# Two-level gates of an attention and feed-forward kernel: another order of the seven products, sums on VectorE, weights' sums at other places

## The chip, the cores and the metric

One core of one Trainium2 chip runs the whole kernel in one launch. The metric is device time in microseconds (us) of an execution, as the median of several runs. TensorE (PE in the profile) multiplies, VectorE (DVE), ScalarE (ACT) and GpSimd (POOL) work on whole tiles, and SyncE (SP) issues most of the transfers.

## The reference

All arrays are float32. Attention without softmax comes first, on 8 batches of 8 heads, 576 tokens and 64 columns; then a feed-forward network on the 4608 tokens.

```python
kv = np.einsum('bhsd,bhse->bhde', k, v)
out = np.einsum('bhsd,bhde->bhse', q, kv)
rms = np.sqrt(np.mean(out * out, axis=-1, keepdims=True) + 1e-06)
x = (out / rms * g_norm)           # heads side by side: 4608 x 512
a = x @ w1                         # 512 x 1024
b = x @ w2                         # 512 x 1024
return ((a * b @ w3) @ w_out)      # 1024 x 1024, then 1024 x 512
```

The kernel multiplies w3 and w_out with each other first, so that only the two gates' products (with w1 and w2) and one product with the folded matrix remain for each token.

## The kernel before

**Groups.** The tokens go through the network in nine groups of 512. Groups 0 to 6 are the first 512 tokens of batches 0 to 6; then comes group 8, the 64 left-over tokens of all batches together, and group 7 is last. Attention for the next group is spread over the current one: a list of steps is called at fixed places (`between`), twice for each of the four quarters `p` of the gate's columns. Places are counted from 0 within a group; at places 1 and 4 stand attention's own products (kv, then q with kv, and the normalisation: L333, L416, L384, L385, L394).

**Products.** Every large product is cut by Winograd's form of Strassen's scheme: seven products of half-size blocks in place of eight, with sums of blocks before (s1 to s4 of the one factor, t1 to t4 of the other) and sums of products behind. In the gates of groups 0 to 6 the scheme is used once (`winograd`, L618). In groups 8 and 7, which `TWICE` names, quarters 0 and 1 of the gates are computed together with the scheme used on two levels (`gates_of_two`, from L824): each of the seven products (`products(n, w, ...)`, L850) is itself seven products of 128 x 128 blocks, kept in two PSUM banks, and the stretch is gone through twice, once for w1 (`w` = 0) and once for w2 (`w` = 1). Quarters 2 and 3 use one level. The product with the folded matrix (`project_twice`, L1049) always uses two.

**The stretch of two levels.** `products(n, ...)` with `new` true starts the banks afresh; with false it adds onto what they hold. Banks are `r1`, `r2` (of five that PSUM keeps under `mm`) and `r3` (of three under `at`). `keep` copies two banks to SBUF by two ScalarE copies (L863, L864); a product that adds onto the same banks has to wait for these copies. `add` is two VectorE additions of banks to a kept tile (L868, L869). `finish` makes one quarter of a gate's block out of seven kept pieces by four VectorE additions (L880 to L883), and in the second pass multiplies it onto the first pass's result (L885). L902 adds the kept `u3` to `p5`.

**What follows.** `sum_ab_two` makes the sums s1, s2, s3, s4 of quarters 0 and 1 as four wide operations of 128 x 512, on GpSimd (L911 to L914). They are needed by `project_twice`. The gates of quarter 3 run at the same time (PE L618; VectorE L757 and L758 once for each of the blocks c12, c22 and c11, L671, L672); behind c11, L1007 to L1011 (`sum_inner`) make the inner sums for the first product of `project_twice`.

**The weights' sums.** The two-level gates need sums of the weights' blocks, seven sets of three (L775, L776, L777: 128 x 256 each, on VectorE). `prepare_w` makes them in groups 3 and 4 and stores each set with three transfers (L780) to `w_l2` in DRAM. It alternates between two buffers, so a set can be written only when the set before the last has been stored. It is called at places 0 to 3 of both groups.

**Who decides the order.** PE, GpSimd and SP run in the order in which the program issues their work. ScalarE's order and, outside of the last quarter and `project_twice` (and `gates_of_two`), VectorE's are arranged by a scheduler. Every engine works its own list strictly in order.

Of the kernel before, what the change touches and what calls it, by code (L numbers as in the profile page):

```python
# [3 lines left out]

# [18 lines left out]
def kernel(  # L23
# [32 lines left out]
    nc = tc.nc  # L56
# [19 lines left out]
    ps_mm = ctx.enter_context(tc.tile_pool(name="ps_mm", bufs=5, space=PSUM))  # L76
# [531 lines left out]
    def late_tile(name):  # L608
        return late_pool.tile([P, 7, P], FP32, name=name[0] if name[0] == "u" else name)
# [214 lines left out]
    def gates_of_two(T):  # L824

        if not places:
            other = work.tile([P, 2, 2, NP // 2, N], FP32, name="xT")
            other = other.rearrange("p i j r n -> p (i j r n)")
            places.extend([other[:, 0:PART // 2], other[:, 1024:1024 + PART // 2]])
            other = work.tile([P, 2, 2, 4, D], FP32, name="xn", bufs=1)  # L830
            places.append(other.rearrange("p i l m d -> p (i l m d)")[:, 0:PART // 2])
            places[:] = [t.rearrange("p (n t) -> p n t", t=P) for t in places]

        def products(n, w, ps, new):
            a_name, b_name = PRODUCTS[n]
            a11, a12, s3, a22 = (t[:, w] for t in w_blocks(a_name))
            s1, s2, s4 = (
                loaded_w[q // 7][:, q % 7 * 2 * P + w * P:q % 7 * 2 * P + (w + 1) * P]
                for q in range(3 * n, 3 * n + 3)
            )  # L840
            b11, _, b21, b22 = (
                xb[T][b_name][:, c, i * P:(i + 1) * P] for c in range(2) for i in range(2)
            )
            t1, t2, t3, t4 = x_sums[n]
            seen = set()
            for place, x, y in (
                (0, a11, b11), (3, a12, b21), (1, a22, t4), (2, s1, t1), (6, s2, t2), (5, s4, b22),
                (4, s3, t3),
            ):
                nc.tensor.matmul(  # L850
                    ps[place // 4][:, place % 4, :], lhsT=x, rhs=y,
                    start=new and place // 4 not in seen, stop=True, skip_group_check=True,
                )
                seen.add(place // 4)
            if w == 1 and n in (2, 4, 6):
                load_b()
            return ps

        def banks(pool, tag):
            return [bank(pool, tag).rearrange("p (i n) -> p i n", n=P) for _ in range(2)]  # L860

        def keep(t, ps):
            nc.scalar.copy(t[:, 0:4], ps[0])  # L863
            nc.scalar.copy(t[:, 4:7], ps[1][:, 0:3])  # L864
            return t

        def add(z, ps):
            nc.vector.tensor_add(z[:, 0:4], ps[0], z[:, 0:4])  # L868
            nc.vector.tensor_add(z[:, 4:7], ps[1][:, 0:3], z[:, 4:7])  # L869

        def finish(z, w, i, j):

            def wide(i):
                return z[:, i:i + 1].to_broadcast([P, 2, P])

            dst = ab[i][:, 0:2, j, :].rearrange("p m (n t) -> p m n t", t=P)
            to = dst
            if w:
                to = late_pool.tile([P, 2, N], FP32, name="c").rearrange("p m (n t) -> p m n t", t=P)
            nc.vector.tensor_add(z[:, 6], z[:, 6], z[:, 0])  # L880
            nc.vector.tensor_add(z[:, 4:6], z[:, 4:6], wide(6))
            nc.vector.tensor_add(to[:, 1], z[:, 1:3], wide(4))  # L882
            nc.vector.tensor_add(to[:, 0], z[:, 3:6:2], z[:, 0:3:2])  # L883
            if w:
                nc.vector.tensor_mul(dst, dst, to)  # L885

        for w in range(2):
            r1 = products(0, w, banks(ps_mm, "mm"), True)
            p1 = keep(late_tile("p1"), r1)
            r3 = products(1, w, banks(ps_at, "at"), True)  # L890
            add(p1, r3)
            finish(p1, w, 0, 0)
            r2 = products(2, w, banks(ps_mm, "mm"), True)
            p5 = keep(places[2] if w else late_tile("p5"), r2)
            products(3, w, r1, False)
            z = keep(late_tile("u2"), r1)
            products(4, w, r2, False)
            add(z, r2)
            finish(z, w, 0, 1)
            products(5, w, r1, False)  # L900
            u3 = keep(places[0], r1)
            nc.vector.tensor_add(p5, p5, u3)  # L902
            finish(p5, w, 1, 1)
            products(6, w, r1, False)
            finish(keep(places[1], r1), w, 1, 0)
        loaded_w.clear()

    def sum_ab_two():
        c11, c12, c21, c22 = (ab[i][:, 0:2, j, :] for i in range(2) for j in range(2))
        s1, s2, s4 = (t[:, 0:2] for t in ab_sums)  # L910
        nc.gpsimd.tensor_add(s1, c12, c22)  # L911
        nc.gpsimd.tensor_sub(s2, s1, c11)
        nc.gpsimd.tensor_sub(c12, c11, c12)
        nc.gpsimd.tensor_sub(s4, c21, s2)  # L914

    def project(T, between):
        def done(name, one, two):
# [96 lines left out]
    def project_twice(T, last, ahead, load_after):  # L1014
# [147 lines left out]
    w3o_l2 = dram.tile([8, P, PART], FP32, name="w3o_l2")  # L1162
    w_l2 = dram.tile([P, 3 * PART], FP32, name="w_l2")
    PRODUCTS = [
        ("a11", "b11"), ("a12", "b21"), ("s1", "t1"), ("s2", "t2"), ("s4", "b22"), ("s3", "t3"),
        ("a22", "t4"),
    ]
    TWICE = (B, B - 1)
# [95 lines left out]
    for n, T in enumerate(groups):  # L1264
        pieces = steps(T + 1) if n + 2 < NG else iter([])

        def between():
            next(pieces, lambda: None)()
            if T == 1:
                for _ in range(2):  # L1270
                    if next(preparing, 0) == 0 and len(loaded_b) < 3:
                        load_b()
            if T in (3, 4) and p < 2:
                next(preparing_w, 0)
            if T == B - 2 and p == 2 and not replaced:
                replaced.append(True)
                replace_a21()

        if T in TWICE:
            once = iter([T])  # L1280
            gates(T, 2, lambda: [sum_x(t) for t in islice(once, 1)])
            run(sum_ab(2))
            in_order = tc.manual_schedule(engines={mybir.EngineType.DVE})
            in_order.__enter__()
            gates_of_two(T)
            sum_ab_two()
        for p in range(NF):
            if T in TWICE and p + 1 < NF:
                continue
            if T and p + 1 == NF:  # L1290
                sum_1, sum_2, sum_4, sum_3 = sum_ab(p)
                following = {
                    "c12": [], "c22": [sum_1],
                    "c11": [
                        lambda: sum_inner(0, lambda: all_of(f() for f in (sum_2, sum_3))),
                        lambda: sum_inner(1),
                    ],
                    "c21": [sum_4],
                }

                if T not in TWICE:
                    in_order = tc.manual_schedule(engines={mybir.EngineType.DVE})
                    in_order.__enter__()
                gates(T, p, between, lambda name: all_of(f() for f in following[name]))
                continue
            gates(T, p, between if T or p else lambda: None)
            if T == 0:
                if p + 1 < NF:
                    run(sum_w(p + 1))
                for n in range(2):  # L1310
                    if len(converted) < len(todo):
                        ahead = [copies["xT"] if p == 0 else copies["u3"][0], copies["u2"][p]][n]
                        with tc.issue_after(ahead.ins):
                            begin_next()
                        end_next()
                if p + 1 == NF:
                    allocate_projection()
                    run(*(f(i) for i in range(NF) for f in (sum_ab, combine_w3o)))
            else:
                run(sum_ab(p))  # L1320
        last = n + 1 == NG
        if T:
            project_twice(
                T, last, [] if last else combine_x(groups[n + 1]),
                load_w if not last and groups[n + 1] in TWICE else load_b,
            )
            in_order.__exit__(None, None, None)
            continue
        project(T, between)
        run(combine_x(1))  # L1330
        preparing, preparing_w, replaced = prepare_b(), prepare_w(), []
        third = late_pool.tile([P, 3, 2, P], FP32, name="inner_sums")
        inner_sums.append([third[:, i] for i in range(3)])
# [30 lines left out]
```

## Time and profile before

| | |
|---|---|
| median of 4 runs | 766.46 us (766.04 to 767.49) |
| the profiled execution | 767.05 us |
| its span in the trace | 765.3 us, so 1.75 us lie around it |
| PE busy | 756.2 us, 99% of the span, granted clock 0.999 |
| VectorE, ScalarE, GpSimd busy | 589.8 us, 263.3 us, 175.8 us |
| stretch of two levels, group 8 | 635.43 to 657.86 us |
| stretch of two levels, group 7 | from 704.46 to 726.89 us |

Times in the trace are counted from the span's start. In a timeline a row is: start, duration, engine, line, operation, output<-inputs, shape, count, and in brackets the engine's idle time before it with what ended it. Durations of neighbours on VectorE overlap a little, so what one operation costs in a queue is the distance from its start to the next start, not its duration. PE has two records for each matmul of float32.

### The profile page before, as it was taken

How to read it: one execution, taken by the hardware profiler on the slowest of the kernel's cores; microseconds unless marked ns; L12 is line 12 of the kernel's file. 1: busy time of each engine (PE TensorE's matmuls, PEld its weight loads, DVE VectorE, ACT ScalarE, POOL GpSimd, SP SyncE). 2: the span in 40 equal slices, each digit the busy share in tenths (PEclk: the TensorE clock that was granted, in tenths of full speed). 3: DMA queues.
4: the chain of work that ended last, by engine and by line, in shares of the span. 5: the costliest groups of instructions: out<-in, count | busy, mean ns of one | idle time of the engine just before them, and what ended most of it. 6: DMA issues, size and time to landing. Idle time of an engine off the chain costs nothing.

```text
span 765.3 us, 15018 instructions
## 1 busy us (share of the span) xinstructions
PE 756.2 (99%) x5943; PEld 661.4 (86%) x5943; DVE 589.8 (77%) x1159; ACT 263.3 (34%) x499; POOL 175.8 (23%) x198
## 2 busy tenths in 40 slices
PE   8999999999999999999999999999999999999998
PEld 6455788888899889988998899889988999999997
DVE  7978999548978468967786688467776778997897
ACT  6677763213221332232222322322223213322421
POOL 0000000222510442044104320431053124206020
PEclk9999999999999999999999999999999999999999
DMA  9996541238998835694569456835642460465234
GB/s 317 340 352 195 185 144 37 84 96 251 330 274 279 233 102 166 213 263 143 167 206 276 118 164 225 223 92 168 227 119 64 152 226 20 147 209 181 95 134 144
DMA packets 137050, 140.84 MB, mean 184 GB/s; under 512 B 77076, under 2 KB 124308, under 8 KB 136980
## 3 DMA queue, kind: packets, MB, share of 16 engines
q1 hardware_dynamic: 134528, 125.46, 54.7%
q10 hardware_dynamic: 2452, 14.42, 5.5%
q8 instruction: 47, 0.77, 0.4%
q14 instruction: 23, 0.19, 0.1%
HBM read 105.78 MB, written 19.14 MB: 163 GB/s over the span
## 4 chain that ended last, share of the span: by engine, by line
PE 81%; issue 6%; DVE 5%; DMA 5%; POOL 2%; ACT 1%; SPq 1%; DVEq 0%; POOLq 0%; ACTq 0%
PE mm L618 44%; PE mm L1049 18%; PE mm L597 7%; PE mm L850 4%; PE at L333 2%; PE at L416 2%; DMA raw<-in_moe_w_out_dram 1%; DMA w3o_sb<-w3o_l 1%; PE at L850 1%; PE at L584 1%; DMA w_l<-raw 1%; DMA xn<-xT 1%; DMA q_sb<-qT 1%; POOL xT L305 1%; DVE c L882 1%
## 5 line engine op out<-in xcount | busy, mean ns | idle before, releaser
L618 PE MATMUL mm<-xT,w_sb 128*128 128x256 f32 x720 | 165.2, 379 | 0.0
L618 PEld LDWEIGHTS mm<-xT,w_sb 128*128 128x128 f32 x720 | 136.3, 190 | 18.7 <-issue 0.5
L618 PE MATMUL mm<-xc,ws 128*128 128x256 f32 x512 | 116.3, 380 | 0.8 <-ACT p L631 0.8
L618 PEld LDWEIGHTS mm<-xc,ws 128*128 128x128 f32 x512 | 96.9, 190 | 14.9 <-ACT p L631 1.8
L631 ACT COPY u<-mm 128x512 f32<-128x512 f32 x66 | 38.6, 585 | 123.6 <-PE mm L618 108.3
L291 POOL COPY xT<-xn 128x1024 uint16<-128x1024 uint16 x26 | 31.0, 1219 | 179.4 <-DVE xn L394 179.4
L757 DVE TENSOR_TENSOR c<-mm,u 128x512 f32<-128x512 f32 x32 | 22.1, 689 | 60.3 <-PE mm L618 59.9
L631 ACT COPY p<-mm 128x512 f32<-128x512 f32 x66 | 38.5, 584 | 73.7 <-PE mm L618 68.0
L597 PE MATMUL mm<-chunks,ab 128*128 128x512 f32 x128 | 60.3, 603 | 1.5 <-DVE chunks L171 1.0
L618 PE MATMUL mm<-xc,w_sb 128*128 128x256 f32 x256 | 61.4, 383 | 0.0
L618 PE MATMUL mm<-xT,ws 128*128 128x256 f32 x240 | 57.3, 382 | 0.0
L758 DVE TENSOR_TENSOR ab<-c 128x256 f32<-128x256 f32 x96 | 53.8, 560 | 2.5
L618 PEld LDWEIGHTS mm<-xc,w_sb 128*128 128x128 f32 x256 | 47.8, 190 | 6.9 <-ACT u L631 0.3
L385 DVE TENSOR_REDUCE inv<-sq 128x8 f32<-128x512 f32 (+1 forms) x40 | 23.4, 626 | 36.0 <-ACT sq L384 36.0
L618 PEld LDWEIGHTS mm<-xT,ws 128*128 128x128 f32 x240 | 44.9, 190 | 6.2
L1049 PE MATMUL mm<-w3o_sb,ab 128*128 128x128 f32 x368 | 49.2, 276 | 0.6 <-DMA w3o_sb<-w3o_l 0.4
L1049 PE MATMUL mm<-w3o_sb,raw 128*128 128x128 f32 x372 | 48.5, 276 | 0.5 <-DVE raw L1007 0.5
L1049 PEld LDWEIGHTS mm<-w3o_sb,ab 128*128 128x128 f32 x368 | 45.5, 192 | 1.7 <-DVE ab L1011 0.6
L1049 PEld LDWEIGHTS mm<-w3o_sb,raw 128*128 128x128 f32 x372 | 44.9, 192 | 0.7 <-DVE raw L1007 0.6
L1060 ACT COPY u<-mm 128x512 f32<-128x512 f32 x23 | 13.5, 586 | 87.2 <-DVE raw L1073 57.5
L305 POOL COPY xT<-xn 128x1024 uint16<-128x1024 uint16 x26 | 30.9, 1216 | 52.6 <-DMA xn<-xT 52.6
L597 PEld LDWEIGHTS mm<-chunks,ab 128*128 128x128 f32 x128 | 21.8, 190 | 24.0 <-issue 15.8
(300 smaller groups left out, 1381.7 us busy)
## 6 DMA issues: line engine op xcount, KB each, us to landing
w3o_sb<-w3o_l SPq DMA_DIRECT2D x18, 896.0 KB, 5.3
raw<-in_moe_w_dram SPq DMA_DIRECT2D x31, 512.0 KB, 7.5
raw<-w3o_l SPq DMA_DIRECT2D x15, 896.0 KB, 4.6
w3o_sb<-w3o_l ACTq DMA_DIRECT2D x14, 896.0 KB, 4.5
k_sb<-in_k_dram SPq DMA_DIRECT2D x32, 256.0 KB, 4.2
v_sb<-in_v_dram SPq DMA_DIRECT2D x32, 256.0 KB, 4.5
q_sb<-in_q_dram SPq DMA_DIRECT2D x32, 256.0 KB, 4.6
out_dram<-raw SPq DMA_DIRECT2D x14, 512.0 KB, 3.6
```

The lines of the kernel that those rows point to most:

```text
L291: nc.gpsimd.tensor_copy(to, src.rearrange("p a n w -> p w a n"))
L305: nc.gpsimd.tensor_copy(words(dst), src)
L333: nc.tensor.matmul(kv_ps[e * D:(e + 1) * D, r - rs[0], :], lhsT=k_sb[:, e, cols] if j < J else kl[:, 2 * r + e, :], rhs=v_sb[:, e, cols] i ...
L385: nc.vector.tensor_reduce(out=inv[:, i], in_=sq.rearrange("p (h d) -> p h d", d=D), axis=AX.X, op=ALU.add)
L416: nc.tensor.matmul(o_ps[l][tokens, n * D:(n + 1) * D], lhsT=qT[r][rows, e, i, tokens], rhs=kv_b[rows, e, r, :], start=True, stop=True,)
L597: nc.tensor.matmul(sums_ps[half][m], lhsT=w3T[half, c][:, m, :], rhs=chunks[:, c, 1, :], start=(c == 0), stop=(c == KF - 1),)
L618: nc.tensor.matmul(ps[:, u, :], lhsT=lhsT(a_name, u, c), rhs=rhs(b_name, c),  start=(u == 0 and c == 0 and to is None), stop=(c == chunks ...
L631: copies.setdefault(name, []).append(nc.scalar.copy(t, ps))
L757: nc.vector.tensor_add(c, one, two)
L758: nc.vector.tensor_mul(dst, c[:, 0, :], c[:, 1, :])
L850: nc.tensor.matmul(ps[place // 4][:, place % 4, :], lhsT=x, rhs=y, start=new and place // 4 not in seen, stop=True, skip_group_check=True,)
L1049: nc.tensor.matmul(to[:, i, :], lhsT=x[:, c, :], rhs=y[:, c, :], start=new and place // 4 not in seen, stop=(c == 1), skip_group_check=True,)
```

## The change

Three things change. (1) Within a pass the seven products come in another order: `s2` x `t2` third (added onto `r1`), `s1` x `t1` fourth (new banks `r2`), `s3` x `t3` fifth (onto `r1`), `s4` x `b22` sixth (onto `r2`), and the last as before (onto `r1`). The banks take turns, and `p5`'s quarter is finished before `z`'s. `PRODUCTS` lists them in this order, so the weights' sets 2 to 5 change their order in DRAM, too. (2) The four wide sums go from GpSimd to VectorE. Two stand behind the stretch's last `finish`, the other two behind quarter 3's c12 and c22. (3) `prepare_w` is called at places 0, 2, 3 and 5 of groups 3 and 4.

```diff
@@ gates_of_two
-            r2 = products(2, w, banks(ps_mm, "mm"), True)
+            products(2, w, r1, False)
+            z = keep(late_tile("u2"), r1)
+            r2 = products(3, w, banks(ps_mm, "mm"), True)
             p5 = keep(places[2] if w else late_tile("p5"), r2)
-            products(3, w, r1, False)
-            z = keep(late_tile("u2"), r1)
-            products(4, w, r2, False)
-            add(z, r2)
-            finish(z, w, 0, 1)
-            products(5, w, r1, False)
+            products(4, w, r1, False)
             u3 = keep(places[0], r1)
             nc.vector.tensor_add(p5, p5, u3)
             finish(p5, w, 1, 1)
+            products(5, w, r2, False)
+            add(z, r2)
+            finish(z, w, 0, 1)
             products(6, w, r1, False)
             finish(keep(places[1], r1), w, 1, 0)
@@ sum_ab_two
-        nc.gpsimd.tensor_add(s1, c12, c22)
-        nc.gpsimd.tensor_sub(s2, s1, c11)
-        nc.gpsimd.tensor_sub(c12, c11, c12)
-        nc.gpsimd.tensor_sub(s4, c21, s2)
+        return [
+            lambda: nc.vector.tensor_add(s1, c12, c22),
+            lambda: nc.vector.tensor_sub(s2, s1, c11),
+            lambda: nc.vector.tensor_sub(c12, c11, c12),
+            lambda: nc.vector.tensor_sub(s4, c21, s2),
+        ]
@@ PRODUCTS
-        ("a11", "b11"), ("a12", "b21"), ("s1", "t1"), ("s2", "t2"), ("s4", "b22"), ("s3", "t3"),
+        ("a11", "b11"), ("a12", "b21"), ("s2", "t2"), ("s1", "t1"), ("s3", "t3"), ("s4", "b22"),
@@ between, in the loop over groups
-            if T in (3, 4) and p < 2:
+            if T in (3, 4) and next(at) in (0, 2, 3, 5):
                 next(preparing_w, 0)
@@ behind gates_of_two(T)
-            sum_ab_two()
+            of_two = sum_ab_two()
+            for _ in range(2):
+                of_two.pop(0)()
@@ quarter 3
-                if T not in TWICE:
+                if T in TWICE:
+                    following["c12"] += of_two[:1]
+                    following["c22"] += of_two[1:]
+                else:
```

More of the change, by code (lines that the diff above doesn't have):

```diff
@@ L1 @@
 from contextlib import ExitStack
-from itertools import islice
+from itertools import count, islice
 from types import SimpleNamespace
@@ L1265 @@
         pieces = steps(T + 1) if n + 2 < NG else iter([])
+        at = count()
         def between():
```

## The prediction

> **What bounds the kernel now.** I read the page's busy times first, then PE's start-to-start distances, then the chain of waits around the first two-level stretch (group 8), and last the timelines of VectorE, GpSimd and PE.
>
> ```profile
> PE 756.2 (99%) x5943; PEld 661.4 (86%) x5943; DVE 589.8 (77%) x1159; ACT 263.3 (34%) x499; POOL 175.8 (23%) x198
> ```
>
> PE is the bound, so the change can win only places where PE stands still. Behind 240 us the timeline has few. In the stretch a matmul record follows the next at 0.1117 us; the larger distances are these, each at the last product of a pass:
>
> ```profile
> 644.59 0.39 PE L850 MATMUL mm<-q_sb,w_sb 128*128 128x128 f32 x2
> 644.98 0.71 PE L850 MATMUL mm<-xc,w_sb 128*128 128x128 f32 x4
> 645.53 0.39 PE L850 MATMUL mm<-qT,w_sb 128*128 128x128 f32 x2
> ```
>
> The first two rows should be 0.22 apart and are 0.39; the four records behind take 0.55 to the next row, where others take 0.45. So the last product waits 0.17 for the copy of the banks that it adds onto, and loses 0.10 more starting up. The second place is the first product of the projection. The chain leads there through VectorE:
>
> ```profile
> 656.97 0.55 issue
> 657.51 1.10 DVE xn L902
> ...
> 661.14 1.47 DVE xT L881
> 662.63 1.38 DVE c L882
> 664.01 1.42 DVE c L883
> 665.45 0.70 DVE ab L885
> ...
> 666.28 0.70 DVE c L757
> 667.00 0.86 DVE ab L758
> ...
> 669.57 0.61 DVE c L757
> 670.20 0.44 DVE ab L758
> ...
> 672.68 0.35 DVE ab L1011
> 673.07 2.94 PE mm L1049 x24
> ```
>
> From the stretch's end to 673.07 VectorE works without a pause, and PE waits for its last sum, L1011. Three additions that take 0.43 elsewhere take about 1.4 here. GpSimd's timeline shows what lies beside them:
>
> ```profile
> 661.05 1.27 POOL L911 TENSOR_TENSOR raw<-ab,ab 128x512 f32<-128x512 f32 x1 [20.43 <-DVE ab L885]
> 662.39 1.33 POOL L912 TENSOR_TENSOR raw<-raw,ab 128x512 f32<-128x512 f32 x1
> 663.69 1.45 POOL L913 TENSOR_TENSOR ab<-ab 128x512 f32<-128x512 f32 x1
> 666.29 1.27 POOL L914 TENSOR_TENSOR raw<-ab,raw 128x512 f32<-128x512 f32 x1 [1.15 <-DVE ab L885]
> ```
>
> The third place is in group 4: VectorE's set of weights' sums waits for a store and holds up attention's reduction, ScalarE's root behind it and the copies behind that.
>
> ```profile
> 408.88 0.88 DVE L775 TENSOR_TENSOR raw<-w_sb 128x256 f32<-128x256 f32 x1 [0.93 <-DMA w_l<-raw]
> 414.95 1.99 PE L618 MATMUL mm<-xc,ws 128*128 128x256 f32 x8 [0.82 <-ACT p L631]
> ```
>
> **Part 1, order of products.** Nothing is added or removed on PE: 98 matmuls at 0.2233 make 21.88, and the stretch takes 657.86 - 635.43 = 22.43. The difference, 0.55, is the two waits with their restarts (2 x 0.27). In the new order another product always stands between a product and the next one onto its banks. The copies of a product's banks end 2.30 after its start (product from 654.46, second copy 656.28 + 0.48 = 656.76); the next product onto them starts two products, 3.13, after it. So these waits go, with 0.8 to spare; the new wait of the third product for p1's copies (637.67) is over when it starts (638.56). PE reaches quarter 3 at 657.31 and the projection, 12.09 later, at 669.40, 0.55 sooner. The weights' loads are laid out in the same order as they are used, so they come when they came.
>
> **Part 2, VectorE's chain.** Before, the unbroken chain begins at 654.06, with L868 behind the fifth product. Now it begins with L902, which needs the kept u3, the copy of the same place's fifth product but through ScalarE: the product starts at 635.43 + 11 x 1.563 = 652.62, its copies end 2.30 later, and L902 starts 0.08 behind them (645.49 to 645.57 in the first pass): 655.00, so 0.94 later. What stands before it in VectorE's queue (the first pass, then p1's quarter) ends at about 654.2 by the same distances, and does not count. The chain up to c11's L757 at 669.48 was 15.42 long. The same additions in another order remain, and of these distances:
> - L881, L882 and L883 beside GpSimd take 4.31 (661.14 to 665.45), without it 1.25 (655.65 to 656.90): minus 3.06.
> - L885 to the next L757 0.83, to an operation that needs nothing of it 0.61 (656.90 to 657.51): minus 0.22.
> - L758 beside L914 0.95, now followed by an independent sum, 0.35 (as L671 to L757): minus 0.60.
> - Four sums of 128 x 512 are added. Independent ones of this size are 0.61 apart, dependent ones (s1 into s2) 0.72 to 0.79 (L661: 676.90 to 677.62, 457.60 to 458.39). So 3 x 0.61 + 0.75: plus 2.58.
>
> 15.42 - 3.88 + 2.58 = 14.12, and c11's L757 comes at 669.12, 0.36 sooner. c22's L757 within it also needs ScalarE's u3, 0.78 + 0.59 behind c12's L757 at 665.31, thus 666.7: over when VectorE arrives (667.0). Behind c11 nothing changes, so L1011's reader on PE starts at 672.71 in place of 673.07. PE itself could be there at 669.40 + 2.68 = 672.08: it now waits 0.63. So PE's 0.55 is given back, and the gain is VectorE's 0.36. Group 7's rows repeat group 8's 69.03 later (L757 at 738.51): 0.36 again. What GpSimd drops covers nothing: it is idle from there to 694.95.
>
> The sums' cost is the uncertain term. At 0.61 each they make 2.44, at 0.79 each 3.16: a gain of 0.50 or a loss of 0.22 for each group. GpSimd's own price for them, 5.32, is the far end. I take 2.58, since the nearest rows are the same form on VectorE. A larger gain would need a 128 x 512 row below 0.61; there is none.
>
> The Trainium skill (VectorE: DVE Perf Modes, "The DRAIN you can't avoid") speaks against the move: the next operation should not start before the pipe of the one before is empty. L902 starts 0.61 behind an L885 of 0.69, so this case's row differs; by the rule the four would cost 4 x 0.69 = 2.76, and the gain would be 0.18 for each group.
>
> **Part 3, weights' sums.** In the built program VectorE's list changes in one place: set 3 in group 3 goes from 342.72 to behind the L672 at 349.96. There VectorE is idle until 355.45 (L385, 4.28 for ScalarE). Three sums at the dearest row, 1.25 beside GpSimd, fit: 351.2 + 3.75 = 354.9. PE does not wait at either place: 0. SP's list: the three stores of sets 1 and 5 go behind two q loads and two transposes of xn each, set 3's behind four k and v loads and four transposes; three stores hold SP 1.54, and those loads wait for GpSimd or PE anyway: 0. The added wait is set 3's for set 1's stores, now issued at 348.14. Stores to w_l land in 1.8 to 6.2, median 3.2; landing by 351.2 costs nothing, at 6.2 L385 would be late, and the price is that of group 4's stall, 0.99 + 0.10 = 1.09. I take 0, as the stores issued at 348.14 before landed in 1.85. In group 4 set 6 keeps its place in VectorE's list, and set 4's stores, which it waits for, keep theirs in SP's (402.80, behind the same loads): the stall stays.
>
> **Sum.** 2 x 0.36 = 0.72 off the profiled 767.05 gives 766.33. That execution lies 0.59 above the median of 766.46; against the median it is 765.74, 0.09% less. A measurement of this kernel can tell about 0.2%, 1.53 us, from no change. With the bounds of the four sums the forecast's own range is 765.4 to 766.9.
>
> **Rivals.**
> 1. Group 4's stall goes, too, because the moved stores leave SP and the transfer engines freer: 1.09 more, 764.65. For it: the wait is only 0.93 long and hangs on a store's landing. Against: neither list changes ahead of it.
> 2. VectorE falls off the path, if its queue overlaps better than the distances say; then PE keeps everything. The first product of the projection would end at 672.53 in place of 673.62: 1.09 for each group, 764.28. Against: the chain would have to be 0.6 shorter still.
> 3. VectorE becomes the worse bound (slower). In quarter 3, the four sums cost there what they cost on GpSimd: 5.32 in place of 2.58, 2 x (2.74 - 0.36) = 4.76 more, 771.2. It decides from 2.94 for the four, 0.74 each. For it: the same stretch already has 1.4 rows. Against: those stand beside GpSimd alone, and L881 takes 0.43 when it rests.
> 4. The change does nothing that lasts: the gain is lost and set 3 waits: 766.46 - 0.72 + 1.09 = 766.83.
>
> **How the numbers follow.** Forecast 0.52, rival 1 0.18, rival 2 0.14, rival 3 0.11, rival 4 0.05. Rivals 1 and 2 lie over 0.2% below: faster 0.32; forecast and rival 4 within: 0.57; rival 3: slower 0.11. The range takes in all but rival 3: 764.2 to 766.9.
>
> **What would show it.** Right: no distance above 0.15 within L850's rows; no GpSimd row in quarter 3; L881 to L883 at 0.43 in every finish; L902 of the second pass at about 655.0, c11's L757 some 11.8 behind quarter 3's first PE row, and PE's wait ahead of the a21 block grown to about 0.6 with its restart; the 0.8 wait of group 4 still there. Wrong: the four sums above 0.74 each, a PE wait near 340 to 360, or group 4's wait gone.

## The result, and the profile after

The changed kernel takes 765.91 us (median of 36 runs, 764.4 to 768.89), the kernel before 766.83 us (55 runs, 764.96 to 769.66). The ratio is 0.9988, 95% interval 0.9983 to 0.9994: 0.9 us faster, between 0.5 and 1.3. That is within the 0.2% named in the prediction. The forecast was a gain of 0.72.

The page of the changed kernel, as before, has PE at 99%. VectorE has eight instructions more and GpSimd eight fewer:

```profile
PE 754.9 (99%) x5943; PEld 660.4 (86%) x5943; DVE 588.1 (77%) x1167; ACT 263.5 (34%) x499; POOL 165.2 (22%) x190
```

VectorE's busy time is lower although it has more to do (589.8 before): its additions no longer lengthen beside GpSimd. PE's timeline at the last product of the first pass, where two rows were 0.39 apart and are now 0.23:

```profile
644.38 0.39 PE L850 MATMUL mm<-q_sb,ws 128*128 128x128 f32 x2
644.61 0.61 PE L850 MATMUL mm<-xc,w_sb 128*128 128x128 f32 x4
645.05 0.39 PE L850 MATMUL mm<-qT,w_sb 128*128 128x128 f32 x2
```

The stretch of two levels takes 21.88 in place of 22.43 (635.23 to 657.11), in group 7 as in group 8. The chain of waits in the same place as before, from u3's addition (now L899) to the projection (now L1051):

```profile
654.75 1.10 DVE xn L899
...
661.76 0.44 DVE xT L881
662.22 0.42 DVE c L882
662.64 0.35 DVE c L883
663.01 0.69 DVE ab L885
663.71 0.61 DVE raw L912
...
666.61 0.70 DVE c L757
...
668.22 0.60 DVE raw L915
668.82 0.61 DVE c L757
...
671.93 0.35 DVE ab L1013
...
672.32 3.73 PE mm L1051 x31
```

The wide sums s1, s2, s3 and s4 now have the lines L912 to L915. L881 to L883 of the last finish take 1.25 in place of 4.31, two of the wide sums stand behind that finish, L914 (left out here) ahead of c22's L757 and L915 ahead of c11's. That last L757 starts, by VectorE's timeline, at 668.74. In group 4 the store still holds up VectorE, as its timeline shows:

```profile
408.84 0.70 DVE L775 TENSOR_TENSOR raw<-w_sb 128x256 f32<-128x256 f32 x1 [1.11 <-DMA w_l<-raw]
```

and PE, by its own timeline, waits as long as before:

```profile
414.74 1.99 PE L618 MATMUL mm<-xc,ws 128*128 128x256 f32 x8 [0.82 <-ACT p L631]
```

The two profiled spans differ by 1.3 (765.3 and 764.0). Of this 1.10 lies in groups 8 and 7, 0.55 each; 0.21 was there at group 4's wait already, ahead of anything the change touches on PE, and belongs to loads in the first 235 us.

### The profile page after: what moved, and what is told of

Same layout as the page of the kernel before. It is cut to its first block, busy times and chain, and to the rows that moved or that the text cites. A ratio compares the mean times of both kernels' runs of the same rounds, so it can differ in the third digit from the quotient of the medians.

```text
span 764.0 us, 15003 instructions
## 1 busy us (share of the span) xinstructions
PE 754.9 (99%) x5943; PEld 660.4 (86%) x5943; DVE 588.1 (77%) x1167; ACT 263.5 (34%) x499; POOL 165.2 (22%) x190
## 4 chain that ended last, share of the span: by engine, by line
PE 82%; issue 6%; DMA 5%; DVE 3%; POOL 2%; ACT 1%; SPq 0%; POOLq 0%; ACTq 0%
PE mm L618 45%; PE mm L1051 18%; PE mm L597 7%; PE mm L850 5%; PE at L333 2%; PE at L416 2%; DMA raw<-in_moe_w_out_dram 1%; DMA w3o_sb<-w3o_l 1%; PE at L850 1%; DMA w_l<-raw 1%; PE at L584 1%; DMA xn<-xT 1%; DMA q_sb<-qT 1%; POOL xT L305 1%; POOL qT L305 1%
## 5 line engine op out<-in xcount | busy, mean ns | idle before, releaser
L631 ACT COPY u<-mm 128x512 f32<-128x512 f32 x66 | 38.7, 587 | 122.6 <-PE mm L618 114.0
L757 DVE TENSOR_TENSOR c<-mm,u 128x512 f32<-128x512 f32 x32 | 22.0, 688 | 60.2 <-PE mm L618 60.2
L631 ACT COPY p<-mm 128x512 f32<-128x512 f32 x66 | 38.5, 585 | 73.7 <-PE mm L618 67.8
L758 DVE TENSOR_TENSOR ab<-c 128x256 f32<-128x256 f32 x96 | 53.8, 560 | 2.5
L1051 PE MATMUL mm<-w3o_sb,ab 128*128 128x128 f32 x368 | 49.2, 276 | 0.4 <-DMA w3o_sb<-w3o_l 0.2
L385 DVE TENSOR_REDUCE inv<-sq 128x8 f32<-128x512 f32 (+1 forms) x40 | 23.4, 626 | 34.0 <-ACT sq L384 34.0
L1051 PE MATMUL mm<-w3o_sb,raw 128*128 128x128 f32 x372 | 48.5, 276 | 0.3 <-DVE raw L1009 0.3
L1051 PEld LDWEIGHTS mm<-w3o_sb,ab 128*128 128x128 f32 x368 | 45.5, 192 | 1.6 <-DVE ab L1013 0.6
L1051 PEld LDWEIGHTS mm<-w3o_sb,raw 128*128 128x128 f32 x372 | 44.9, 192 | 0.6 <-DVE raw L1009 0.5
```

What stands on the lines that cost most here:

```text
L385: nc.vector.tensor_reduce(out=inv[:, i], in_=sq.rearrange("p (h d) -> p h d", d=D), axis=AX.X, op=ALU.add)
L631: copies.setdefault(name, []).append(nc.scalar.copy(t, ps))
L757: nc.vector.tensor_add(c, one, two)
L758: nc.vector.tensor_mul(dst, c[:, 0, :], c[:, 1, :])
L1051: nc.tensor.matmul(to[:, i, :], lhsT=x[:, c, :], rhs=y[:, c, :], start=new and place // 4 not in seen, stop=(c == 1), skip_group_check=True,)
```

## Experiments

The question was why PE's 0.55 in the stretch arrived whole, where 0.36 was forecast, and which part made it. One measure serves for all kernels. Q is the start of quarter 3's first PE row. The a21 block is PE's third block of the projection's first product (the row at 672.32 above, which waits for L1013). From the traces of group 8:

| kernel | stretch | c11's L757 behind Q | PE's a21 block of the projection behind Q | ratio to before, 95% interval |
|---|---|---|---|---|
| before | 22.43 | 11.62 | 15.21 | |
| changed | 21.88 | 11.63 | 15.21 | 0.9988 (0.9983 to 0.9994) |
| part 1 alone | 21.88 | 12.97 | 16.55 | 1.0025 (1.0016 to 1.0034) |
| part 2 alone | 22.42 | 11.58 | 15.16 | 1.0004 (0.9996 to 1.0013) |
| part 3 alone | as before | | | 0.9999 (0.9991 to 1.0008) |
| three buffers | as changed | | | 0.9995 (0.9986 to 1.0003) |
| s4 late | 21.88 | 11.02 | 14.77 | 0.9968 (0.9958 to 0.9979) |
| s3 late | 21.88 | 11.59 | 15.16 | 0.9980 (0.9967 to 0.9993) |
| set in group 5 | as changed | | | 0.9972 (0.9963 to 0.9981) |
| s4 late, set in group 5 | 21.88 | 11.02 | 14.77 | 0.9954 (0.9942 to 0.9966) |
| the same, old order | 22.43 | 10.98 | 14.76 | 0.9968 (0.9956 to 0.9980) |

PE alone needs 12.09 + 2.68 = 14.77 to the a21 block, so the last column but one less 14.77 is what PE loses on the way there: 0.44 in the changed kernel, a wait of 0.07 with its restart of 0.10 in the first block, and a wait of 0.27 ahead of a21. Behind a21 another restart of 0.10 follows.

### The three parts one by one

**Part 1 alone** (the hunks of `gates_of_two` and `PRODUCTS`).

> Part 1 alone: the new order of the seven products; the four wide sums stay on GpSimd and the weights' sums at their old places. Theory A (the parts need each other): PE loses its waits in the stretch (0.55 a group), but VectorE's unbroken chain now begins 0.94 later, with the addition of u3, and its last finish still stands beside GpSimd's sums (three additions at about 1.4 instead of 0.43). The c11 addition of quarter 3 then comes some 13.0 behind quarter 3's first PE row instead of 11.62, about 0.8 later than before in absolute terms, and PE waits for it: slower than before by 2 x 0.8 = 1.6 us, about 768.4. Theory B (the parts add up, the order of the products is what wins): faster by 2 x 0.55 = 1.1, about 765.7. Theory C (PE's waits in the stretch are all made good elsewhere): same as before.

Measured: 768.69 against 766.58, 1.2 to 2.6 slower. Theory A holds: c11's L757 is 12.97 behind Q where 13.0 was expected. VectorE's timeline shows the finish beside GpSimd's sums, as before the change:

```profile
660.73 1.46 DVE L881 TENSOR_TENSOR xT<-xT 128x256 f32<-128x256 f32 x1
662.22 1.37 DVE L882 TENSOR_TENSOR c<-xT 128x256 f32<-128x256 f32 x1
663.52 1.48 DVE L883 TENSOR_TENSOR c<-xT 128x256 f32<-128x256 f32 x1
```

PE's timeline shows two new waits: one in quarter 3, for its u3 (ScalarE's L631, not the kept u3 of the stretch), and one for c11's L758:

```profile
667.28 1.99 PE L618 MATMUL mm<-xc,w_sb 128*128 128x256 f32 x8 [0.67 <-ACT u L631]
...
670.26 0.94 PE L1049 MATMUL mm<-w3o_sb,ab 128*128 128x128 f32 x6 [0.31 <-DVE ab L758]
```

By the table PE has 0.55 less in the stretch and 1.34 more behind it, +0.79 for a group and +1.58 for both.

**Part 2 alone** (the hunks of `sum_ab_two`, behind `gates_of_two` and in quarter 3).

> Part 2 alone: the four wide sums on VectorE, the products in the old order, the weights' sums at their old places. Theory A: VectorE's chain is 1.3 shorter by its operations, but in quarter 3 it is caught by PE: c22's addition needs ScalarE's copy u3, which ends 9.43 behind quarter 3's first PE row in the changed kernel; quarter 3 starts as late as before, so c11's addition comes at about the same time as before (0.03 to 0.1 sooner). Gain 0.1 to 0.2 us in all: no difference that can be measured, about 766.7. Theory B (the parts add up): the 1.1 us is the order's, so no difference or a loss of up to 0.2. Theory C (the sums alone make the gain, since VectorE sets PE's wait): PE's 0.44 a group falls away, 0.9 faster, about 765.9.

Measured: 766.86 against 766.58, no difference. VectorE's operations are shorter, but it now stands still twice in quarter 3, as VectorE's timeline shows:

```profile
664.62 0.69 DVE L757 TENSOR_TENSOR c<-mm,u 128x512 f32<-128x512 f32 x1 [0.62 <-PE mm L618]
...
666.90 0.69 DVE L757 TENSOR_TENSOR c<-p,u 128x512 f32<-128x512 f32 x1 [0.52 <-ACT u L631]
```

The second of these ties c11 to PE: c22 cannot be added sooner than about 9.46 behind Q (666.90 - 657.44). So what the sums' move as made here saves in VectorE's chain is worth next to nothing alone, 0.05 for a group. Theory C is out.

**Part 3 alone** (the hunk of `between`).

> Part 3 alone: the weights' sums at places 0, 2, 3 and 5, nothing else. Theory A: 0; PE's start-to-start distances in groups 3 and 4 are those of before, the wait of about 0.99 in group 4 is still there, since the sixth set still waits in VectorE's list for a store. Theory B: the stores that are issued later leave room, and part of the 1.09 goes: 765.8 to 766.6.

Measured: no difference (0.9991 to 1.0008), which alone would not part the two theories. PE's distance in group 4 does: it is 0.989 over the usual one, before 0.986, so nothing of it went. In the changed kernel the added wait of set 3 for a store is there, 0.65 long, and ends in VectorE's idle time: three sums until 352.2, the reduction L385 at 355.24 after 3.02 of idling.

So the parts do not add up. The order alone costs 1.6 by the traces, the sums' move alone brings 0.1, and together they bring 1.1.

### Which sum counts

The fourth sum, s4, is moved behind c21:

```diff
-                    following["c22"] += of_two[1:]
+                    following["c21"] = of_two[1:] + following["c21"]
```

> The changed kernel with the last of the four sums (s4, L915) moved from ahead of c11's addition to behind the product c21, where the projection still has three products to go before it needs it. Theory A (c22's addition is tied to ScalarE's copy u3, 9.5 behind quarter 3's first PE row, and what stands in VectorE's queue behind it sets PE's wait at the projection): c11's addition comes 11.0 behind quarter 3's first PE row in place of 11.63, PE's wait of 0.44 a group (0.07 + 0.27 + 0.10) falls away whole, 0.9 faster than the changed kernel, about 765.0, 1.8 faster than before. Theory B (PE's own order sets the 0.27, not VectorE's queue): no difference from the changed kernel.

In the other kernel it is the third sum, s3, that goes behind c21, while s4 stays ahead of c11:

```diff
-                    following["c12"] += of_two[:1]
+                    following["c21"] = of_two[:1] + following["c21"]
```

> The changed kernel with the third of the four sums (L914, of the same size) moved behind the product c21 instead, the others in their places. Theory A: L914 stands ahead of c22's addition, which waits for u3's copy in any case (the copy ends 0.07 before it); VectorE will idle 0.5 to 0.6 there, c11's addition stays 11.6 behind quarter 3's first PE row, and the time is that of the changed kernel, 765.9. Theory B (VectorE's queue as a whole sets the wait, so that any 0.6 less counts): 0.9 faster, about 765.0.

In this kernel L914 reads c11 after L1013 has overwritten half of what it reads with a difference, so s3 holds another value; shapes and lists are the same.

Measured: 764.03 (1.6 to 3.2 faster than before) with s4 late, 765.61 (0.5 to 2.5 faster) with s3 late. These intervals overlap; the traces tell the two apart. The same 0.60 of VectorE work counts in one place and not in the other. With s4 late PE goes through without a wait; the a21 block, which followed 1.61 behind the row ahead of it, follows by 1.34:

```profile
668.27 1.50 PE L1051 MATMUL mm<-w3o_sb,ab 128*128 128x128 f32 x12
669.61 1.50 PE L1051 MATMUL mm<-w3o_sb,raw 128*128 128x128 f32 x12
670.95 0.61 PE L1051 MATMUL mm<-w3o_sb,ab 128*128 128x128 f32 x4
```

With s3 late VectorE idles where s3 was, and c11 is 0.04 sooner in group 8 and no sooner in group 7 (11.64 behind Q with and without the edit). VectorE's timeline of group 8:

```profile
666.64 0.69 DVE L757 TENSOR_TENSOR c<-p,u 128x512 f32<-128x512 f32 x1 [0.47 <-ACT u L631]
```

s4 late brings 0.54 for a group by the traces, 0.44 of waiting and 0.10 of restart ahead of the next block, where 0.44 was expected: the expectation had left one of two restarts out.

### The wait in group 4

The changed kernel with three buffers in `prepare_w`:

```diff
-            s1, s2, s4 = inner_sums[2 * (n % 2)]
+            s1, s2, s4 = inner_sums[n % 3]
```

> The changed kernel with three buffers in turn for the weights' sums instead of two (the third is one that the projection's inner sums use between the groups' ends), so that no set of group 4 waits for a store of the same group. Theory A (the 0.99 of group 4 comes from VectorE's wait for the store of set 4, with attention's reduction queued behind it): the wait and its restart go, 1.09 faster than the changed kernel, about 764.8, and 2.0 faster than before. Theory B (the reduction is late because of the GpSimd copies beside it, which lengthen the additions to 1.25): at most 0.3 faster than the changed kernel.

Measured: 765.82, 0.9986 to 1.0003 of before, so no gain over the changed kernel. The stall is gone, as Theory A has it: PE has no wait at 413. But the scheduler, which has a free buffer now, puts three sets in place of two into the tails of the projections ahead of groups 3 and 4. The finish L1075 there comes later, ScalarE's copy p1 waits for it, and PE for the copy (PE's timeline):

```profile
323.64 1.99 PE L618 MATMUL mm<-xc,ws 128*128 128x256 f32 x8 [0.50 <-ACT p L631]
...
399.84 1.99 PE L618 MATMUL mm<-xc,ws 128*128 128x256 f32 x8 [0.50 <-ACT p L631]
```

Each of these is 0.66 over the usual distance, where the changed kernel has 0.04 and 0: 1.28 lost for 1.09 won. In the changed kernel the same copy follows L1075 too, but 0.6 sooner, and PE loses no more than a restart. To take the wait away without filling those tails, the last set goes to group 5 instead, with two buffers:

```diff
-            if T in (3, 4) and next(at) in (0, 2, 3, 5):
+            if T in (3, 4, 5) and next(at) in ((0, 2, 3, 5), (0, 3), (0,))[T - 3]:
```

> The changed kernel with two sets of weights' sums in group 4 (places 0 and 3) and the last one at place 0 of group 5; two buffers as before. No set waits for a store of its own group, and no group's end holds more than two sets. Theory A (group 4's 0.99 is the wait for the store; the 0.66 at the starts of groups 3 and 4 in the kernel with three buffers came from three sets in the tail of the projection ahead, where the changed kernel has two): the stall goes and nothing comes in its place, 1.09 faster than the changed kernel, about 764.8. Theory B (whatever is moved comes back elsewhere): some other wait of 0.6 or more, and within 0.4 of the changed kernel.

Measured: 764.38, 1.5 to 2.8 faster than before. PE's rows of group 4 are whole (x16 where there were x8 and a wait), and no new distance appears in groups 3 to 5. VectorE's reduction now waits for ScalarE, not behind a store:

```profile
408.71 1.28 DVE L385 TENSOR_REDUCE inv<-sq 128x8 f32<-128x512 f32 x2 [0.70 <-ACT sq L384]
```

Both kernels take the whole set out of this stage. So the wait for the store is not tested apart from the set's own three additions, nor apart from Theory B of the kernel with three buffers: in the changed kernel two additions L672 behind the wait stand beside GpSimd's copies and take 1.25 each, here 0.43 and 0.42. That the wait came first and pushed them there is read from the rows, not tested.

### Both, and the old order again

The changed kernel with the edits of s4 late and of the set in group 5 together:

> s4 behind the product c21 and the last set of weights' sums in group 5, both on the changed kernel. Theory A: the two lie in different stages and add up, 0.9 + 1.1 = 2.0 faster than the changed kernel, about 763.9, ratio to before 0.996. Theory B: as much as the better of the two alone, about 764.8.

Measured: 762.98 against 766.84, 2.6 to 4.4 faster than before. This is the fastest kernel here. By the traces it is 1.09 x 2 + 1.09 = 3.27 faster, so by the traces Theory A holds; the interval still overlaps that of s4 late alone.

That kernel without the hunks of `gates_of_two` and `PRODUCTS`:

> The kernel with s4 behind c21 and the last set in group 5, but with the seven products in the old order. Theory A (the order's 0.55 a group is PE's own and counts whole once VectorE's queue no longer sets the projection's start): PE has its four waits of 0.17 with their restarts of 0.10 in the stretches again, no wait at the projection, and is 4 x 0.27 = 1.1 slower than the same kernel in the new order: 764.1, ratio to before about 0.997. Theory B (the order brings little in any case, as part 2 with the old order suggested): within 0.3 of the kernel in the new order, 763.0.

Measured: 764.54 against 766.96, 0.9956 to 0.9980. The stretch's waits are back, 0.169, 0.170, 0.168 and 0.168 over the usual distance, and the projection has none. By the traces 1.08 slower than the new order; the two ratios are 0.0014 apart, which is 1.1, though their intervals overlap. With VectorE off the path, the order of the products counts in full.

## Why the prediction was right, by its steps

**Part 1, right.** The stretch's 0.55 was predicted and is 0.55 in both groups. No distance above 0.15 is left in L850's rows, and the projection starts 12.09 behind Q as predicted.

**Part 2, right in mechanism, 0.19 too dear.** L881 to L883 fell by the 3.06 that was put down, L885 to the next row is 0.61, and L758 to the sum behind it 0.34 (0.35 was put down). The four sums cost 0.72 + 0.61 + 0.60 + 0.60 = 2.53; 2.58 had been put down. The mis-sized terms are small ones: 0.05 for the sums; 0.05 at the start, where L899 follows the copy by 0.03 and not by 0.08 (the row that gave 0.08, at 645.57, has no idle time before it, so VectorE's queue set it and not the copy); 0.07 that was not put down at all, L868 to L869, which are 0.67 apart where L868 had waited (before) and 0.60 apart in a running queue (658.07 to 658.67). The remaining 0.02 is rounding. Together they make 0.19 for a group, the difference between 0.36 and 0.55. Two signs did not come: the grown wait (next but one paragraph), and L881 and L882 at 0.43 in every finish. In the first finish of the first pass they take 0.56 beside GpSimd's additions, before the change as after it.

**The number, in part luck.** The forecast time of 765.74 lies 0.17 from the measured 765.91, nearer than its terms were. Its base, the median of 4 runs, was 0.37 below the 766.83 of 55 runs, and its gain of 0.72 was 0.20 below the measured 0.92 (0.38 below the 1.10 of the traces). The two errors cancel in part.

**What was late next, only half seen.** The prediction gave PE's wait at the projection as grown to 0.6. It stayed 0.44. It also let c22's L757 arrive 0.3 behind quarter 3's copy u3. It arrives within 0.1 of it: the copy ends at 665.95 + 0.59 = 666.54, L757 starts at 666.61. The copy's time was right, 9.4 behind Q in the prediction and in the trace, but not what it waits for. The prediction hung it 0.78 behind c12's L757, as in the kernel before; ScalarE's timeline shows it waiting for PE's product:

```profile
665.95 0.59 ACT L631 COPY u<-mm 128x512 f32<-128x512 f32 x1 [2.87 <-PE mm L618]
```

So the chain had reached the point at which PE, through ScalarE, binds it again: a further saving ahead of c22 is worth 0.05 at most, as the kernel with s3 late showed. The prediction has no such tie; in it, a shorter chain ahead of c22 would have gone on paying.

**Part 3, right.** 0, with the wait of set 3 for set 1's store as described and covered; group 4's stall stayed.

**The drain rule** of the Trainium skill (VectorE: DVE Perf Modes, "The DRAIN you can't avoid") was weighed against L902's row and gave way. In the changed kernel independent sums of 0.68 to 0.69 start 0.60 to 0.61 apart. The prediction had read half of the rule: the same section says that a next operation that is not held starts earlier. Read whole, the section does not ask for the full 0.69 of each sum, and these rows do not speak against it.

**The rivals.** Group 4's stall did not go (rival 1). VectorE did not leave the path by this change (rival 2), and s4's place is what kept it there; with s4 late the cap of 1.09 for a group that rival 2 named was reached. The sums stayed at 0.60 to 0.72 (rival 3 needed 0.74). Rival 4's wait of set 3 came and was covered.

## What to carry to other kernels

When two engines wait in turn, ask for each saving which engine it is on and which event ties the two together next: here the new order of the products was worth 0.55 for a group with the sums off GpSimd and cost 0.79 with them there. The sums' move as made brought 0.05 without the order; with s4 behind c21 as well, PE's wait at the projection went in the old order, too (14.76 in the table's last row). An operation ahead of a wait that stays is free, up to the length of that wait, and one behind it delays all that follows by its full distance, so in an engine's own list look for what the next reader does not yet need and put it behind. A freed buffer or place can also be taken up by the scheduler, as with three buffers here, so see in the built order where work goes before counting a removed wait as gained.

## What the runs showed of the hardware

An addition of 128 x 256 on VectorE with both inputs in SBUF takes 0.42 alone and 1.37 to 1.48 beside GpSimd's sums of 128 x 512. In the kernel with part 1 alone GpSimd's rows are these (GpSimd's timeline):

```profile
660.64 1.27 POOL L911 TENSOR_TENSOR raw<-ab,ab 128x512 f32<-128x512 f32 x1 [21.25 <-DVE ab L885]
661.99 1.33 POOL L912 TENSOR_TENSOR raw<-raw,ab 128x512 f32<-128x512 f32 x1
663.28 1.44 POOL L913 TENSOR_TENSOR ab<-ab 128x512 f32<-128x512 f32 x1
```

They end at 661.91, 663.32 and 664.72; the three additions shown above end at 662.19, 663.59 and 665.00, each 0.27 or 0.28 later. So each looks as if it had been held until the GpSimd operation beside it ended. The rows around GpSimd's fourth sum (GpSimd's timeline, then VectorE's) bear this out:

```profile
665.88 1.27 POOL L914 TENSOR_TENSOR raw<-ab,raw 128x512 f32<-128x512 f32 x1 [1.15 <-DVE ab L885]
...
665.87 0.69 DVE L757 TENSOR_TENSOR c<-mm,u 128x512 f32<-128x512 f32 x1
666.59 0.84 DVE L758 TENSOR_TENSOR ab<-c 128x256 f32<-128x256 f32 x1
```

L758, with both inputs in SBUF, starts in the middle of L914 and ends at 667.43, 0.28 behind L914's end at 667.15. It takes 0.84, so in these rows the price is what is left of the GpSimd operation, not a factor on VectorE's own time. L757, which takes one input from PSUM, keeps its 0.69 beside L914. The Trainium skill (SBUF — State Buffer, "Who interferes with whom") says that a VectorE instruction with two SBUF inputs contends with a GpSimd instruction that reads SBUF, and that one with at most one SBUF input, outside the 2-port perf modes, does not; these rows agree.

PE loses about 0.10 after each wait, whether the wait was 0.17 long (the stretch before the change) or 1.1 (part 1 alone, group 7). So a wait that goes brings its length and 0.10: at the projection the waits of 0.07 and 0.27 went with s4 late, and 0.54 was won.
